# adaLN block: later modulation vectors by four row sums in column groups and a spread over memory

## Chip, core and metric

The kernel runs on one core of a Trainium2 chip. The metric is device time in microseconds. Each engine of the core works through its own instruction stream in order: TensorE (PE for its products, PEld for its weight loads), VectorE (DVE), ScalarE (ACT), GpSimd (POOL) and SyncE (SP), which here issues nearly all transfers (DMAs). Streams wait for one another through semaphores.

## The reference

```python
x = A_x                                               # 1 x 2048 x 512, float32
mod = (_silu(c) @ w_mod).reshape(c.shape[0], 6, 1, -1)  # c: 1 x 512, w_mod: 512 x 3072
sa, ca, ga, sb, cb, gb = (mod[:, i] for i in range(6))
h = _layernorm(x, axis=-1) * (1 + ca) + sa
x = x + ga * _A_ref(h, A_wqkv, A_wo)                  # 32 heads of 16, softmax attention, then wo
h = _layernorm(x, axis=-1) * (1 + cb) + sb
x = x + gb * _B_ref(h, B_w1, B_b1, B_w2)              # 512 -> 1792, mish, 1792 -> 512
```

Six modulation vectors of 512 come out of one row-by-matrix product. `sa` and `ca` (numbers 0 and 1) are needed at once; the other four (2 `ga`, 5 `gb`, 3 `sb`, 4 `cb`) only later, and they are what is changed here.

## The kernel before

**Stages.** A prologue loads x, makes vectors 0 and 1, normalises, transposes and starts the q, k, v products. Then comes the attention, 512 steps (`T`) written out by hand in `step(t)`: 32 iterations (4 blocks of 512 queries by 8 groups of 4 heads) of 16 steps, one for each block of 128 keys. The row maxima run 20 steps (`PRO`) ahead of the scores. A step puts on PE four score products (L587, exponentiated by ACT at L590), four products for maxima (L538, reduced by DVE at L540), a share of a larger product that is cut into halves of 64 rows (L138), and at its end the four products of probabilities and values of two steps before, `pv` (L605, eight instructions, since a float32 product is two). Scores and maxima go through a ring of six PSUM banks. After the steps a tail finishes the last block.

**Order.** Everything is in program order on its engine; there is no scheduler. `at(h, f)` hangs work on half step h (two to a step), which sets its place in the program order of each engine, not a time. `units` are products fed into the steps; `specials` are done whole in one place: `do_specials` emits a special's products between the step's score products and its `pv`, and its `fin` one half step later. The built program also makes each transfer of SP wait until the eighth transfer before it has landed.

**The later vectors.** `order = (2, 5, 3, 4)`; call them the first to the fourth. For each, `mod_load` (L696) loads two halves of its columns of `w_mod` (128 x 4 x 256, 512 KB) into two buffers (`hl`, `wm`), and POOL multiplies by silu(c) and adds the four blocks of rows (`sums`, L703 to L705), which leaves 128 x 256 values to be summed over the partitions. `mod_unit` (L709) does that on PE, at L131. For a gate (2, 5) it multiplies a 128 x 128 block of ones with each half, so that every partition has the whole vector, and ACT copies it to `gates` (L722). For 3 and 4 it takes each 128 columns as weights and ones as a single moving column, so that the vector lies over the partitions, and DVE copies it to `modc` (L724, L726). `queue_mod` chains the four: the special of a vector is ready 6 half steps after the place of its second `sums`; its `fin` calls `first_mods`, which issues both loads of the next vector, with the `sums` 7 and 9 half steps on. After the fourth, `start_preps` takes over the two buffers and scales and splits the later weights; the gates are read there (L737), `modc` in the second half of the block (L922, L1146).

The names in the profile: `wm` are the loads, `ring` the banks, `qscr`, `kscr`, `vscr` scratch tensors in memory for q, k and v, `sm`, `od`, `rc` the sums and rows of a finished iteration (`evac`, L613), `mt` the rows of maxima.

Of the kernel before, what the change touches and what calls it, by code (L numbers as in the profile page):

```python
# [8 lines left out]
F32 = mybir.dt.float32  # L9
F32R = mybir.dt.float32r  # L10
AF = mybir.ActivationFunctionType
# [7 lines left out]
def adaln_block(ctx: ExitStack, tc: tile.TileContext, x, wqkv, wo, w1, b1, w2, c, w_mod, out):  # L19
    nc = tc.nc  # L20
    P = 128
    S, D = x.shape[1], x.shape[2]
# [3 lines left out]
    DK = D // P  # L26
# [27 lines left out]
    dram = ctx.enter_context(tc.tile_pool(name="dram", bufs=1, space=DRAM))  # L54
# [18 lines left out]
    ones = cst.tile([P, 1], F32, name="ones")  # L73
# [9 lines left out]
    modc = cst.tile([P, 4, DK], F32, name="modc")  # L83
    sil = cst.tile([P, DK], F32, name="sil")
    b1c = cst.tile([P, FT], F32, name="b1c")
    gates = [cst.tile([P, D], F32, name=f"gate{i}") for i in range(2)]

    def dap(t, off, ap):
        return bass.AP(tensor=t.tensor, offset=t.offset + off, ap=ap)
# [36 lines left out]
    def mm(acc, l, r, start, stop):  # L126
        pe_queue.append((acc, l, r, start, stop))
# [27 lines left out]
    def ring(w=1):  # L155
        if w == 2 and ring_at[0] % 2:
            ring_at[0] += 1
        if kept and ring_at[0] % NRING == NRING - 1:
            ring_at[0] += 1
        b = ring_at[0] % NRING  # L160
        ring_at[0] += w
        return ring_t[:, b, :] if w == 1 else ring_t[:, b:b + 2, :]
# [41 lines left out]
    def at(h, f):  # L204

        hooks.setdefault(h, []).append(f)
# [121 lines left out]
    with ExitStack() as es:  # L328
# [121 lines left out]
        for i in range(2):  # L450
            row = lp.tile([P, D], F32, tag="hf", name="row", bufs=6)
# [159 lines left out]
    st, mst = {}, {}  # L611
# [84 lines left out]
    def mod_load(i, h):  # L696

        w = pw.tile([P, DK, 2 * P], F32, tag="hl", name="wm", bufs=2)
        nc.sync.dma_start(w, w_mod[:, i * 2 * P:(i + 1) * 2 * P].rearrange("(k p) m -> p k m", p=P))
        mst["wm", i] = w  # L700

        def sums():
            nc.gpsimd.tensor_mul(w, w, sil[:, :, None].to_broadcast([P, DK, 2 * P]))  # L703
            nc.gpsimd.tensor_add(w[:, 0:2], w[:, 0:2], w[:, 2:4])
            nc.gpsimd.tensor_add(w[:, 0], w[:, 0], w[:, 1])  # L705
            mst["row at", i] = h + 7
        at(h + 7, sums)

    def mod_unit(v):  # L709

        gate = v in (2, 5)
        acc, rows = ring(), [mst.pop(("wm", 2 * v + o))[:, 0] for o in range(2)]
        for o, row in enumerate(rows):
            if gate:
                mm(acc[:, o * 2 * P:(o + 1) * 2 * P], ones.to_broadcast([P, P]), row, True, True)
            else:
                for m in range(2):
                    mm(acc[:, 2 * o + m:2 * o + m + 1], row[:, m * P:(m + 1) * P], ones, True, True)

        def fin(h):  # L720
            if gate:
                nc.scalar.copy(gates[(v - 2) // 3], acc)  # L722
            elif v == 4:
                nc.vector.tensor_scalar_add(modc[:, v - 1, :], acc[:, :DK], 1.0)  # L724
            else:
                nc.vector.tensor_copy(modc[:, v - 1, :], acc[:, :DK])  # L726
        return fin

    def prep_unit(h, third, scr, src, gate):
# [666 lines left out]
    def planned(i, a, tag):  # L1396
        _, kind, sl, args = plan[i]
        unit = v_unit(sl, a, tag) if kind == 2 else qk_unit(kind, sl, a, tag)

        def fin(h):  # L1400
            if a == args[-1]:
                if i + 2 < len(plan):
                    d = 4 if h > 0 else 1
                    split_at[i + 2] = LATE_SPLIT.get(i + 2, h + d)
                    at(split_at[i + 2], lambda: slice_split(*plan[i + 2][1:3], hi_eng="p" if h > 0 else "a"))
                if i + 3 < len(plan):
                    at(LATE_LOAD.get(i + 3, h + 7), lambda: slice_load(*plan[i + 3][1:3]))
            unit(h)
            if (kind, sl, a) == (2, 0, NKC - 1):
                at(max(0, h + 2), lambda: first_mods(max(0, h + 2)))  # L1410
            if i + 1 == len(plan) and a == args[-1]:
                mst["qkv"] = h // 2 + 3
        return fin

    at(-2 * PRO, lambda: slice_load(*plan[2][1:3]))
    order = (2, 5, 3, 4)

    def first_mods(h, j=0):
        for o in range(2):
            mod_load(2 * order[j] + o, h + 2 * o)  # L1420

    def queue_mod(j):
        def make():
            put = mod_unit(order[j])

            def fin(h):
                put(h)
                if j + 1 < len(order):
                    first_mods(h, j + 1)
                else:  # L1430
                    start_preps(h + 2)
            return fin

        queue_special(lambda: mst.get(("row at", 2 * order[j] + 1), 4 * T) + 6, make)
# [110 lines left out]
```

## Time and profile before

| | |
|---|---|
| median of 3 runs | 1696.19 us (1695.32 to 1696.70) |
| the profiled execution | 1695.12 us, its span 1693.1 us |
| PE, DVE, ACT, POOL busy | 99%, 85%, 80%, 49% of the span |
| products of the four vectors (L131) start at | 123.93, 148.19, 172.28, 196.50 us |
| transfers over the span | 238.44 MB, 141 GB/s |

A row of a timeline gives start, length, engine, line, operation, tiles and count, and in brackets the idle time before it with what ended it. A row of the chain of waits gives the start, the length and the group that the end hung on. Lines such as L131 are lines of the kernel before.

### The profile page before, as it was taken

What the parts mean: (1) busy time and instruction counts of PE and PEld (TensorE: products, weight loads), DVE (VectorE), ACT (ScalarE), POOL (GpSimd) and SP (SyncE); (2) the same over time, 40 slices, a digit from 0 to 9 for tenths busy, and PEclk for the clock granted to TensorE, in tenths of its full rate; (3) what the DMA queues carried; (4) which work ended last, traced back from release to release, by engine and by line L of the source; (5) the groups of instructions that cost most, each with busy time, mean ns of one, the idle gap of its engine ahead of it and who ended that gap; (6) DMA issues with size and microseconds to landing.
All of it is one profiled execution on the core that took longest, in us unless ns stands there. A gap on an engine that the chain in (4) does not pass through costs nothing.

```text
span 1693.1 us, 33733 instructions
## 1 busy us (share of the span) xinstructions
PE 1670.7 (99%) x12406; PEld 922.2 (54%) x12406; DVE 1443.6 (85%) x2371; ACT 1356.1 (80%) x2610; POOL 822.3 (49%) x843
## 2 busy tenths in 40 slices
PE   7999999999999999999999999999999999999999
PEld 5755665555445455555555455555555445555587
DVE  8888888888889898888889898888889888884377
ACT  6257777777778988888888998888888988888674
POOL 7555224665313564555323564556323565555443
PEclk9999999999999999999999999999999999999999
DMA  7877546777755443434355534534354433433261
GB/s 248 264 241 202 130 131 186 225 222 215 225 161 142 107 100 87 125 82 131 88 139 148 118 76 94 140 75 128 83 147 123 130 93 77 143 107 129 76 230 63
DMA packets 114029, 238.44 MB, mean 141 GB/s; under 512 B 23824, under 2 KB 49424, under 8 KB 107912
## 3 DMA queue, kind: packets, MB, share of 16 engines
q1 hardware_dynamic: 113864, 236.28, 49.4%
q8 instruction: 98, 1.61, 0.4%
q14 instruction: 67, 0.55, 0.1%
HBM read 179.95 MB, written 51.44 MB: 137 GB/s over the span
## 4 chain that ended last, share of the span: by engine, by line
PE 91%; DVE 4%; ACT 3%; DMA 1%; issue 1%; POOL 1%; SPq 0%; ACTq 0%; DVEq 0%; POOLq 0%
PE bk L605 29%; PE ring L587 22%; PE ring L538 20%; PE bk L138 10%; PE bk L131 3%; PE ring L131 2%; DVE mx L540 2%; PE ring L1214 2%; ACT pr L590 1%; PE ring L552 1%; DMA qa<-mt 0%; DMA xt<-in_A_x 0%; PE ring L917 0%; PE ring L567 0%; PE ring L138 0%
## 5 line engine op out<-in xcount | busy, mean ns | idle before, releaser
L540 DVE TENSOR_REDUCE mx<-ring 128x1 f32<-128x512 f32 x1968 | 1222.1, 681 | 151.7 <-PE ring L538 136.4
L590 ACT ACTIVATE pr<-ring 128x512 f32<-128x512 f32 x2048 | 1078.3, 603 | 207.8 <-PE bk L138 117.9
L538 PE MATMUL ring<-ka,qa 64*128 64x512 f32 x1968 | 818.6, 429 | 1.7 <-ACT pr L590 1.1
L587 PE MATMUL ring<-qa,ka 64*128 64x512 f32 x2048 | 760.1, 402 | 4.3 <-ACT pr L590 2.6
L605 PE MATMUL bk<-pr,vg 128*32 128x512 f32 x4096 | 545.0, 604 | 0.0
L538 PEld LDWEIGHTS ring<-ka,qa 64*128 64x128 f32 x1968 | 350.5, 184 | 327.4 <-DVE mx L540 250.8
L587 PEld LDWEIGHTS ring<-qa,ka 64*128 64x128 f32 x2048 | 373.6, 184 | 199.2 <-DVE mx L540 115.2
L138 PE MATMUL bk<-h,w 64*128 64x512 f32 (+1 forms) x1080 | 278.6, 391 | 0.0
L138 PE MATMUL bk<-w,a_h 64*128 64x512 f32 x632 | 210.7, 413 | 0.0
L138 PEld LDWEIGHTS bk<-h,w 64*128 64x128 f32 x1080 | 178.3, 184 | 9.5 <-ACT pr L590 1.5
L605 PEld LDWEIGHTS bk<-pr,vg 128*32 128x32 f32 x4096 | 80.7, 108 | 136.1 <-issue 126.6
L138 PE MATMUL bk<-w,a_l 64*128 64x512 f32 x316 | 124.2, 393 | 0.0
L138 PEld LDWEIGHTS bk<-w,a_h 64*128 64x128 f32 x632 | 106.9, 184 | 2.7
L973 POOL TENSOR_TENSOR y<-yd,y 128x512 f32<-128x512 f32 x44 | 56.9, 1293 | 89.6 <-ACT yd L972 84.7
L807 POOL TENSOR_SCALAR qq<-ee 128x512 f32<-128x512 f32 x25 | 15.6, 624 | 168.9 <-ACT ee L801 168.9
L823 POOL TENSOR_TENSOR qq<-qq,rr 128x512 f32<-128x512 f32 x42 | 54.3, 1292 | 83.8 <-ACT rr L817 83.6
L809 POOL TENSOR_TENSOR hb<-hb,ee 128x512 f32<-128x512 f32 x42 | 54.1, 1289 | 82.3 <-DVE ee L805 80.4
L138 PE MATMUL bk<-w,o_hl 64*128 64x512 f32 x288 | 79.1, 404 | 0.0
L100 POOL TENSOR_TENSOR a_l<-hb,a_h 128x512 fp32r<-128x512 f32 x53 | 72.2, 1363 | 4.4
L97 POOL TENSOR_SCALAR qh<-qf 128x512 fp32r<-128x512 f32 x27 | 16.8, 623 | 88.7 <-ACT qf L261 69.7
L138 PEld LDWEIGHTS bk<-w,a_l 64*128 64x128 f32 x316 | 58.3, 185 | 2.9
L138 PE MATMUL bk<-h_h,wl 64*128 64x512 f32 x168 | 56.9, 420 | 0.0
(222 smaller groups left out, 1916.8 us busy)
## 6 DMA issues: line engine op xcount, KB each, us to landing
ka<-kscr SPq DMA_DIRECT2D x124, 384.0 KB
w<-w2scr SPq DMA_DIRECT2D x56, 512.0 KB
w<-w1scr SPq DMA_DIRECT2D x46, 512.0 KB
vg<-vscr SPq DMA_DIRECT2D x32, 552.0 KB
qa<-qscr SPq DMA_DIRECT2D x124, 100.0 KB
kscr<-qh SPq DMA_DIRECT2D x16, 512.0 KB
qscr<-qh SPq DMA_DIRECT2D x32, 256.0 KB
w2scr<-hl SPq DMA_DIRECT2D x14, 512.0 KB
```

What stands on the lines that cost most here:

```text
L100: (nc.gpsimd if eng == "p" else nc.vector).tensor_sub(lo, src, hi.bitcast(F32))
L131: nc.tensor.matmul(acc, l, r, start=start, stop=stop)
L138: i = nc.tensor.matmul(acc, l[64 * g:64 * g + 64], r[64 * g:64 * g + 64], start=start and not then, stop=bool(stop and then))
L538: nc.tensor.matmul(pm, qt[64 * s:64 * s + 64, qs * P:(qs + 1) * P], kt[64 * s:64 * s + 64, kb * TB:(kb + 1) * TB], start=True, stop=True)
L540: nc.vector.tensor_reduce(out=mxs[n][:, s, 4 * j + qs, kb:kb + 1], in_=pm, op=ALU.max, axis=AX.X)
L587: nc.tensor.matmul(p_, kt[64 * s:64 * s + 64, kc * P:(kc + 1) * P], qt[64 * s:64 * s + 64, :], start=True, stop=True)
L590: e = nc.scalar.activation(pr, p_, AF.Exp, scale=SCALE)
L605: nc.tensor.matmul(accs[n][32 * h:32 * h + 32, :], vgs[n][:, o:o + 32], pts.pop((t, h)), start=(kc == 0), stop=(kc == 15))
L809: (nc.vector if tail else nc.gpsimd).tensor_mul(hb, hb, ee)
L823: nc.gpsimd.tensor_mul(qq, qq, rr)
L973: nc.gpsimd.tensor_add(y[i], yd, y[i])
L1214: nc.tensor.matmul(po[i // 2][:, i % 2, :], l[:, s], w[:, r, :], start=(f == 0 and j == 0), stop=(f == FT - 1 and j == 2))
```

## The change

All four vectors are now summed in the same way: four products with a 128 x 32 block of ones, each with 128 columns, put their results side by side into the four groups of 32 partitions of one bank. ACT copies the 128 x 128 result into the second weight buffer (`modt`), for number 4 with one added. Two half steps later one row of each group (4 x 512 bytes) is stored to a scratch tensor in memory; five half steps after `fin` a second transfer reads it back, to all 128 partitions for a gate, or element by element into a column of `modc`. The second buffer is thereby in use until the store has read it, and the second load of the next vector is put 4 half steps later than before; the place of its `sums` stays where it was. In the built program PE, POOL and DVE keep their order otherwise, ACT has two copies more, DVE two fewer, SP eight transfers more.

```diff
+    mscr = dram.tile([4, DK, P], F32, name="mscr")
...
     def mod_unit(v):
-        gate = v in (2, 5)
-        acc, rows = ring(), [mst.pop(("wm", 2 * v + o))[:, 0] for o in range(2)]
-        for o, row in enumerate(rows):
-            if gate:
-                mm(acc[:, o * 2 * P:(o + 1) * 2 * P], ones.to_broadcast([P, P]), row, True, True)
+        acc, ws = ring(), [mst.pop(("wm", 2 * v + o)) for o in range(2)]
+        rows, modt = [w[:, 0] for w in ws], ws[1][:, 1, :P]
+        for c in range(DK):
+            mm(acc[32 * c:32 * c + 32, :P], ones.to_broadcast([P, 32]), rows[c // 2][:, c % 2 * P:(c % 2 + 1) * P], True, True)
+
+        def fin(h):
+            if v == 4:
+                nc.scalar.activation(modt, acc[:, :P], AF.Identity, bias=ones)
             else:
-                for m in range(2):
-                    mm(acc[:, 2 * o + m:2 * o + m + 1], row[:, m * P:(m + 1) * P], ones, True, True)
-
-        def fin(h):
-            if gate:
-                nc.scalar.copy(gates[(v - 2) // 3], acc)
-            elif v == 4:
-                nc.vector.tensor_scalar_add(modc[:, v - 1, :], acc[:, :DK], 1.0)
-            else:
-                nc.vector.tensor_copy(modc[:, v - 1, :], acc[:, :DK])
+                nc.scalar.copy(modt, acc[:, :P])
+            dst = mscr[v - 2]
+
+            def spread():
+                if v in (2, 5):
+                    nc.sync.dma_start(gates[(v - 2) // 3], dap(dst, 0, [[0, P], [1, D]]))
+                else:
+                    nc.sync.dma_start(modc[:, v - 1, :], dst.rearrange("k p -> p k"))
+
+            at(h + 2, lambda: nc.sync.dma_start(dst, modt[::32, :]))
+            at(h + 5, spread)
         return fin
...
     def first_mods(h, j=0):
-        for o in range(2):
-            mod_load(2 * order[j] + o, h + 2 * o)
+        mod_load(2 * order[j], h)
+        at(h + 4, lambda: mod_load(2 * order[j] + 1, h + 2))
```

## The prediction

> **What bounds the kernel now.** I read the page first, then the chain of waits around the four places that change, then the timelines of POOL and SP there.
>
> ```profile
> span 1693.1 us, 33733 instructions
> PE 1670.7 (99%) x12406; PEld 922.2 (54%) x12406; DVE 1443.6 (85%) x2371; ACT 1356.1 (80%) x2610; POOL 822.3 (49%) x843
> PE 91%; DVE 4%; ACT 3%; DMA 1%; issue 1%; POOL 1%; SPq 0%; ACTq 0%; DVEq 0%; POOLq 0%
> ```
>
> PE is busy throughout and carries 91% of the chain; so what PE is spared or made to wait in a step moves the end by as much. The chain around the first vector, with one ordinary step on either side:
>
> ```profile
> 121.04 0.99 PE bk L605 x8
> ...
> 123.93 1.10 PE ring L131 x4
> 125.03 0.99 PE bk L605 x8
> ...
> 127.87 1.00 PE bk L605 x8
> ```
>
> From one `pv` to the next an ordinary step takes 127.87 - 125.03 = 2.84 us; the step with the vector takes 3.99, longer by its 1.10 us of L131 and little else. The second, third and fourth cost nearly the same:
>
> ```profile
> 148.19 1.09 PE ring L131 x4
> ...
> 172.28 1.02 PE ring L131 x8
> 173.30 1.00 PE bk L605 x8
> ...
> 196.50 1.02 PE ring L131 x8
> ```
>
> Together 4.23 us lie on the path; that is all that the new products can save.
>
> **The products.** Each vector now takes four products of 128 columns in four column groups, eight instructions. The nearest row is `pv` itself, eight instructions in the same groups with 512 columns, 0.99 us on the chain. A quarter of that is 0.25 us, the lower bound. The upper bound is the same number of 128-column instructions that share nothing:
>
> ```profile
> L684 PE MATMUL ring<-ident,wide 128*64 128x128 f32 x8 | 1.1, 279 | 0.0
> ```
>
> 1.1 us, which would be no gain. I take 0.35, close to `pv`: its form is the same, and 0.1 is added for the issue, because the third product has a wait of its own for the second `sums`. Saved: 0.75 + 0.74 + 0.67 + 0.67 = 2.83 us, between 0 and 3.2.
>
> **The copies.** ACT loses two long copies and gets four short ones, DVE loses two:
>
> ```profile
> L722 ACT COPY gate<-ring x2: 616/622/627, 125.2 to 149.5; 128x512 f32<-128x512 f32 x2
> L922 ACT ACTIVATE hf<-ring,modc x48: 450/464/484, 518.0 to 1297.5; 128x128 f32<-128x128 f32 x48
> L724 DVE TENSOR_SCALAR modc<-ring x1: 163/163/163, 197.6 to 197.6; 128x4 f32<-128x4 f32 x1
> L737 POOL TENSOR_TENSOR hl<-hl,gate x18: 1270/1286/1299, 292.7 to 450.8; 128x512 f32<-128x512 f32 x18
> ```
>
> At the 128 x 128 price of L922, four copies are 1.86 us against 1.24 before. Both engines have room beside PE (80% and 85%), so nothing reaches the path: 0, at worst 0.46 in each of the last two vectors' steps if that room is gone. The spreads have some 100 us and more before the gates (292.7) and `modc` (518.0) are first read: 0 both ways.
>
> **The moved load.** This is what decides. The second load of the next vector now waits on SP until the store of the vector before has landed, since the store reads the same buffer; what is queued behind it on SP waits too. For the third vector, before (SP's timeline, and a load's size from the transfers' list; then POOL's timeline):
>
> ```profile
> 149.56 0.94 SPq L699 DMA_DIRECT2D wm<-in_w_mod  x2
> ...
> 157.83 0.57 SPq L271 DMA_DIRECT2D qscr<-ql  x1
> 161.03 0.59 SPq L630 DMA_DIRECT2D sm<-ot  x1
> ...
> 172.92 0.93 SPq L699 DMA_DIRECT2D wm<-in_w_mod  x2
> ...
> wm<-in_w_mod SPq DMA_DIRECT2D x3, 512.0 KB
> ```
>
> ```profile
> 157.90 1.89 POOL L703 TENSOR_TENSOR wm<-wm,sil 128x1024 f32<-128x1024 f32 x1 [4.78 <-PE ring L538]
> ...
> 161.92 1.89 POOL L703 TENSOR_TENSOR wm<-wm,sil 128x1024 f32<-128x1024 f32 x1
> ...
> 165.25 0.74 POOL L705 TENSOR_TENSOR wm<-wm 128x256 f32<-128x256 f32 x1
> 177.03 1.90 POOL L703 TENSOR_TENSOR wm<-wm,sil 128x1024 f32<-128x1024 f32 x1 [11.04 <-DMA wm<-in_w_mod]
> ```
>
> Both loads went out at 149.56; POOL had the first at 157.90 (8.3 us: a backlog), the second by 161.92, and finished its `sums` at 165.99 (4.07 us of work), 6.3 us before PE wanted them at 172.28. With empty queues a load takes 177.03 - 172.92 = 4.1 us. In the new order the store of the second vector stands right behind qscr<-ql on SP. How long does a transfer there take?
>
> ```profile
> SPq L641 <- DMA qscr<-ql: 1.0, 1, 1.0
> SPq L630 <- DMA wm<-in_w_mod: 2.6, 1, 2.6
> L641 SPq EVENT_SEMAPHORE  x30: 17/17/17, 169.0 to 1558.9; - x30
> ```
>
> These are waits of SP between 147 and 178 us. The last wait ended at 169.0, when qscr<-ql landed, 11.2 us after its issue; and sm went out (161.03) when the second load had landed. The queue of the transfers is drained in order, and it was full:
>
> ```profile
> DMA  0169699799999999999999765655665799930100
> GB/s 0 43 195 316 151 211 240 243 265 214 137 162 124 199 345 351 378 173 175 139 186 217 148 176 170 202 158 202 227 227 202 225 284 306 291 98 6 12 0 0
> ```
>
> That is 147 to 173 us in slices of 0.65: no gap until about 170. So the small store lands where qscr<-ql did, less what the second load, now behind it, no longer takes ahead of it: 512 KB are 1.5 us at the 351 GB/s of the fastest slices, and about 3.1 by the two landings (157.9 and 161.0). The store lands at 169.0 - 1.5 to 3.1 = 165.9 to 167.5, say 166.8. The load follows, 4.1 us: 170.9. `sums`, 4.07: 175.0. PE is there at 172.28 less the 1.49 saved at the first two vectors: 170.8. It stands in front of the third product for 4.2 us, with `pv`, the next scores and thereby ACT and DVE behind it. The last two products take some 0.2, `pv` starts at 175.2 instead of 173.30: 1.9 us late. The fourth vector gives 0.67 back. Sum: +1.3 us; by the bounds of the store's landing +0.4 to +2.0. Since the stall ends when the load says, what the products save at the first two vectors is swallowed by it; at 1.1 us a vector the sum would be +2.4, at 0.25 it would be +1.1.
>
> The other three hold. First: its store does not stand in the way of a load of its own; its second load only goes out two places later. POOL's rows for the first two vectors, and two of SP's:
>
> ```profile
> 117.97 1.90 POOL L703 TENSOR_TENSOR wm<-wm,sil 128x1024 f32<-128x1024 f32 x1
> ...
> 121.31 0.73 POOL L705 TENSOR_TENSOR wm<-wm 128x256 f32<-128x256 f32 x1
> ...
> 139.45 1.90 POOL L703 TENSOR_TENSOR wm<-wm,sil 128x1024 f32<-128x1024 f32 x1
> ...
> 125.60 0.80 SPq L312 DMA_DIRECT2D qa<-qscr  x2
> ...
> 141.26 2.67 SPq L576 DMA_DIRECT2D qa<-mt  x4
> ```
>
> POOL took it up at 117.97 only because it had other work, and ended 1.9 us before PE came at 123.93. Second: the second `sums` started at 139.45, 8.7 us before PE at 148.19. Its load now waits for the first store, behind the transfers issued from 125.60 on; by the same reckoning it lands within a us of 139.45. Margin some 3 us. Fourth: from 172.92 on the queue is nearly empty; load, store, load give POOL its data at about 185, PE comes at 196.50. Cost 0 in all three, up to 2 each if a margin is wrong.
>
> Behind the waiting load on SP stands sm, for whose data DVE divides:
>
> ```profile
> 170.41 0.24 DVE L640 RECIPROCAL rc<-sm 128x16 f32<-128x16 f32 x1
> ```
>
> sm now lands behind the load, at about 171.5, and DVE, which would be there at 168.9, waits 2.6 us, PE with it. That wait lies inside the 4.2 us and is not added.
>
> The profiled execution took 1695.12 us (its span and 2.0 around it); +1.3 makes 1696.4. The median of the runs is 1.07 above that execution: 1697.5.
>
> **Rivals.** *The store overtakes the backlog.* It has four pieces of 512 bytes, on few of the transfer engines. If these are ahead of the others, it lands at about 160, the load joins the backlog and lands at 168 at the latest; `sums` end at 172.1, the stall is 1.3: -2.83 + 1.3 = -1.5 us, 1694.7; with no stall at all -2.8, 1693.4. Against: qscr<-ql took 11.2 us in that queue. [...] Only if the products cost no more than 0.25 and nothing stalls does it come near -3.2.
>
> *PE loses its clock in the stall* (slower). At the start, after long idleness, the same form ran slower:
>
> ```profile
> L448 PE MATMUL ring<-wma,sil 128*32 128x512 f32 x16 | 3.6, 1061 | 9.2 <-DVE sil L363 9.2
> L605 PE MATMUL bk<-pr,vg 128*32 128x512 f32 x272 | 36.2, 605 | 0.0
> ```
>
> 1061 ns against 605, though the row of the granted clock is full over the whole span:
>
> ```profile
> PEclk9999999999999999999999999999999999999999
> ```
>
> If two waits of over 2 us within 6 bring that back for the 3.6 us that it lasted there at least, the price is some 1.8, for 7 us 3.5: +3.1 to +4.8, take +4: 1700.2. [...]
>
> *A second transfer comes late* (slower): the rows of maxima for the second iteration, issued from 141.26 us, now stand behind the second vector's load, a vg load and the gate. If they miss the scores by 2 to 3 us, or the third vector's store lands 2.5 later than said, the end is +3.3 to +4.3: 1700.
>
> **Numbers.** What a measurement can tell from no change is about 0.2%, 3.4 us. Forecast (stall at the third vector, -0.5 to +3) 0.55; overtaking or no stall 0.17; clock 0.12; second late transfer 0.16. Faster by over 0.2% needs the products at their floor and no stall: 0.06 out of the second case. Slower by over 0.2%: 0.10 of the clock, 0.12 of the late transfer, 0.05 of the forecast's tail, 0.27. Within: 0.67. The range leaves out the far end of both sides: 1693.3 (no stall) to 1701.0.
>
> **What would show it.** Right: L131 about 0.35 us on the chain for the first, second and fourth vector; at the third a POOL wait for the load ending at about 171 and a PE wait for `sums` of about 4 us (shared with DVE waiting for sm); from there on ordinary steps. Wrong: L131 near 1 us (the products do not share), no PE wait near 171 to 175, a wait at another vector, matmuls of 1 us after the stall, or ACT named before the scores of the last two vectors' steps.

## The result, and the profile after

| | median | lowest to highest | ratio to before, 95% interval |
|---|---|---|---|
| before | 1695.8 us (15 runs) | 1694.16 to 1699.32 | 1 |
| changed | 1699.74 us (15 runs) | 1697.41 to 1702.0 | 1.0022 (1.0015 to 1.0029) |

The change costs 3.9 us by the medians; 1697.5 was predicted, with a range up to 1701.0. The profiled execution took 1699.35 us, its span 4.5 us more than before. One of the twelve runs of one kernel below (product later) took 3750.89 us and is left out of its median. The page after:

```profile
span 1697.6 us, 33767 instructions
PE 1668.8 (98%) x12414; PEld 919.7 (54%) x12414; DVE 1444.2 (85%) x2369; ACT 1355.9 (80%) x2612; POOL 820.7 (48%) x843
PE 91%; DVE 4%; ACT 2%; DMA 2%; POOL 1%; issue 1%; SPq 0%; ACTq 0%; POOLq 0%; DVEq 0%
```

PE is busy for 1.9 us less (1670.7 before) in a span 4.5 us longer: it stands still for some 6 us more. The chain of waits around the first vector (start, length, group; L132 and L606 are L131 and L605 of before):

```profile
121.18 1.02 PE bk L606 x8
...
124.10 0.42 PE ring L132 x8
124.52 0.86 PE bk L606 x8
...
127.22 1.00 PE bk L606 x8
```

Two steps take 127.22 - 121.18 = 6.04 us; before, 127.87 - 121.04 = 6.83. The products went from 1.10 to 0.42, and `pv` behind them is 0.13 shorter: 0.79 us saved at this vector. So what the change is built of works, and the loss is elsewhere. SP's timeline, from the first vector to the third:

```profile
127.67 0.58 SPq L730 DMA_DIRECT2D mscr<-wm  x1
137.05 0.37 SPq L700 DMA_DIRECT2D wm<-in_w_mod  x1
...
158.98 0.57 SPq L272 DMA_DIRECT2D qscr<-ql  x1
161.67 0.52 SPq L730 DMA_DIRECT2D mscr<-wm  x1
168.60 0.40 SPq L700 DMA_DIRECT2D wm<-in_w_mod  x1
169.10 0.60 SPq L631 DMA_DIRECT2D sm<-ot  x1
```

and the waits of SP between 120 and 172 us (total, times, longest):

```profile
SPq L700 <- DMA mscr<-wm: 15.1, 2, 8.7
```

Both second loads stand on SP until the store of the vector before has landed: 8.7 us the first time, 6.4 the second. The store is 2 KB; it lands 9.4 and 6.9 us after its issue. Both times the transfer engines have just run dry: their busy share is 0.02 between 136 and 137 us and 0.00 in the next, 0.10 between 168.0 and 168.6 and 0.00 from there to 169.5. What follows, in POOL's timeline and then in PE's (in brackets the idle time before, and what ended it):

```profile
141.33 1.89 POOL L704 TENSOR_TENSOR wm<-wm,sil 128x1024 f32<-128x1024 f32 x1 [2.49 <-PE ring L539]
...
172.37 1.89 POOL L704 TENSOR_TENSOR wm<-wm,sil 128x1024 f32<-128x1024 f32 x1 [6.55 <-DMA wm<-in_w_mod]
...
175.68 0.72 POOL L706 TENSOR_TENSOR wm<-wm 128x256 f32<-128x256 f32 x1
```

```profile
170.10 0.39 PE L588 MATMUL ring<-qa,ka 64*128 64x512 f32 x1
170.13 0.40 PE L139 MATMUL bk<-wh,h_l 64*128 64x256 f32 x2
173.22 0.79 PE L588 MATMUL ring<-qa,ka 64*128 64x512 f32 x1 [2.69 <-DVE mx L541]
...
176.45 0.43 PE L132 MATMUL ring<-wm,ones 128*32 128x128 f32 x2 [1.86 <-POOL wm L706]
```

PE stands still from 170.5: first for DVE, then, after 1.4 us of scores and the first two products, for the `sums`. The waits between 165 and 186 us name what held DVE:

```profile
DVE rc L641 <- DMA sm<-ot: 3.3, 1, 3.3
...
PE ring L588 <- DVE mx L541: 2.7, 1, 2.7
```

That is sm, which stood behind the waiting load on SP. Then the chain behind the stall:

```profile
168.60 3.61 DMA wm<-in_w_mod
172.37 1.90 POOL wm L704
...
176.45 0.43 PE ring L132 x2
176.88 0.21 PE bk L606
177.09 1.71 PE bk L606 x6
178.80 0.72 PE ring L588
...
181.06 0.99 PE bk L606 x8
...
183.95 1.00 PE bk L606 x8
```

From 181.06 to 183.95 a step takes 2.89 us again, but the one before took 181.06 - 176.88 = 4.18, with matmuls at half rate (1057 ns for one of `pv`, 605 before): 1.3 us more. The windows show it; the number behind POOL's is the granted clock:

```profile
170.00:172.00 2.00, 0.53 (x8) 0.33 (x4) 0.00 (x0) 1.52 (x4) 0.00 (x0) 1.00 0.97 279
172.00:174.00 2.00, 0.78 (x4) 0.34 (x6) 1.63 (x4) 0.00 (x0) 1.63 (x1) 0.71 0.53 170
174.00:178.00 4.00, 2.14 (x18) 0.70 (x16) 0.96 (x2) 0.86 (x2) 2.24 (x3) 0.50 0.75 187
178.00:180.00 2.00, 2.00 (x14) 1.18 (x12) 0.41 (x1) 0.44 (x1) 0.00 (x0) 0.59 0.95 307
180.00:182.00 2.00, 2.00 (x24) 1.03 (x21) 2.00 (x4) 1.72 (x4) 1.46 (x1) 1.00 0.20 71
```

Stretches with one clock throughout read 1.00 (170 to 172, 180 to 182) or 0.50 (174 to 178). With these two values alone, a mean of 0.71 in two microseconds puts the fall at 172.84, and 0.59 the return at 179.64: by this estimate 6.8 us at half rate. Of these PE had work in 173.2 to 174.6, which the stall covered, and from 176.45 on, which it did not.

### The profile page after: what moved, and what is told of

Read it like the earlier page. It is cut to its first block, busy times and chain, and to the rows that moved or that the text cites. A ratio compares the mean times of both kernels' runs of the same rounds, so it can differ in the third digit from the quotient of the medians.

```text
span 1697.6 us, 33767 instructions
## 1 busy us (share of the span) xinstructions
PE 1668.8 (98%) x12414; PEld 919.7 (54%) x12414; DVE 1444.2 (85%) x2369; ACT 1355.9 (80%) x2612; POOL 820.7 (48%) x843
## 4 chain that ended last, share of the span: by engine, by line
PE 91%; DVE 4%; ACT 2%; DMA 2%; POOL 1%; issue 1%; SPq 0%; ACTq 0%; POOLq 0%; DVEq 0%
PE bk L606 29%; PE ring L588 22%; PE ring L539 19%; PE bk L139 10%; PE bk L132 3%; DVE mx L541 2%; PE ring L1219 2%; PE ring L132 2%; ACT pr L591 1%; PE ring L553 1%; DMA xt<-in_A_x 0%; PE ring L922 0%; DMA qa<-mt 0%; PE ring L568 0%; DMA qscr<-ql 0%
## 5 line engine op out<-in xcount | busy, mean ns | idle before, releaser
L606 PE MATMUL bk<-pr,vg 128*32 128x512 f32 x4096 | 546.4, 605 | 0.0
L606 PEld LDWEIGHTS bk<-pr,vg 128*32 128x32 f32 x4096 | 81.5, 108 | 135.6 <-issue 126.0
```

Of the source, the lines that this page charges most:

```text
L606: nc.tensor.matmul(accs[n][32 * h:32 * h + 32, :], vgs[n][:, o:o + 32], pts.pop((t, h)), start=(kc == 0), stop=(kc == 15))
```

## Experiments

The theory: the products save what was said; the loss is the wait of a load for the store out of the same buffer, and the clock that falls in the stall. Rivals: the later place of the load alone; the new transfers themselves; the products.

| kernel | median | ratio to before, 95% interval | first to fourth vector |
|---|---|---|---|
| gate tile as staging, load late | 1695.77 us | 1.0000 (0.9991 to 1.0009) | 71.85 us |
| gate tile as staging, both loads together | 1693.64 us | 0.9986 (0.9978 to 0.9995) | 70.24 us |
| the same on a second chip | 1693.92 us | 0.9987 (0.9978 to 0.9996) | 70.23 us |
| changed, stores issued by ACT | 1696.31 us | 1.0004 (0.9995 to 1.0013) | 72.49 us |
| before, with store and late load | 1700.93 us | 1.0032 (1.0020 to 1.0043) | 78.76 us |
| changed, sm ahead of the load | 1703.87 us | 1.0049 (1.0037 to 1.0061) | 79.84 us |
| the same, PE kept busy | 1700.16 us | 1.0032 (1.0021 to 1.0043) | 77.94 us |
| changed, product later | 1698.50 us | 1.0019 (1.0010 to 1.0028) | 85.05 us |
| product later and sm ahead | 1694.15 us | 0.9992 (0.9984 to 1.0001) | 81.73 us |
| gate tile, products four times | 1695.46 us | 0.9998 (0.9989 to 1.0007) | 72.19 us |
| gate tile, no gate store or spread | 1692.67 us | 0.9982 (0.9973 to 0.9990) | 70.21 us |
| changed, on that second chip | 1699.55 us | 1.0022 (1.0011 to 1.0033) | 77.42 us |

Rows 1, 2, 4 and 5 were measured on one chip, rows 6 to 9 on another, and the rest on the one called the second chip; each ratio is to the kernel before on the same chip (1695.49, 1695.2 and 1695.54 us). The last column is the start of the fourth vector's product less that of the first in the profiled execution: 72.57 before, 77.31 in the changed kernel. It leaves out what executions of one kernel differ by ahead of the first vector and behind the fourth. In rows 8 and 9 the third product stands later, so that they compare only with each other.

**The wait and the place of the load.** First the buffer alone:

```diff
-        rows, modt = [w[:, 0] for w in ws], ws[1][:, 1, :P]
+        rows = [w[:, 0] for w in ws]
+        modt = gates[(v - 2) // 3][:, :P] if v in (2, 5) else ws[1][:, 1, :P]
```

> The changed kernel, but the vectors 2 and 5 are staged for their store in the gate tile that their spread fills later, not in the second buffer: no load waits for a store any more in front of the second and third vector, while the second load stays four half steps late. Theory A (the wait of the load on the store makes the loss): no stall at the third vector, 1692.7 us (1695.8 less 3.1). Theory B (the later place of the load is itself enough, since the load now stands behind qscr<-ql in a full queue): the load lands at about 169.5, the sums end at about 173.5, PE stands 2 to 3 us: 1694.5 to 1696. Theory C (stores and spreads on the transfer queue cost by themselves): near 1699.

Measured 1695.77: theory B by the time, though PE stands for less than the 2 to 3 us said. Its chain and its PE timeline:

```profile
160.96 7.34 DMA wm<-in_w_mod
```

```profile
172.53 0.30 PE L132 MATMUL ring<-wm,ones 128*32 128x128 f32 x2 [1.26 <-POOL wm L706]
```

Without the wait the load goes out 7.6 us earlier than in the changed kernel (160.96, not 168.60), but into the full queue: it takes 7.34 us instead of 3.61, and PE still stands for 1.3 us. So most, not all, of the loss was the wait; the place takes a part. By the last column, 5.5 us of the way from 77.31 to the 70.24 of the next kernel come with the wait (and the clock that falls in it), 1.6 with the place. Then the place too:

```diff
-        at(h + 4, lambda: mod_load(2 * order[j] + 1, h + 2))
+        if j < 3:
+            mod_load(2 * order[j] + 1, h + 2)
+        else:
+            at(h + 4, lambda: mod_load(2 * order[j] + 1, h + 2))
```

> As the run before, and both loads of the second and third vector are issued together as in the kernel before. Theories A and B: no PE wait near 171 to 176, the products keep their saving of about 0.79 us a vector: 1692.7 us, ratio to before 0.998. Theory C: the transfers of the stores and spreads cost what the products save or more: 1695.8 or above.

Measured 1693.64, faster than both kernels; on the second chip 1693.92:

> The kernel with the gate tile as staging and both loads together once more, on the chip of these runs: 1.8 to 3.1 us below before, faster than both kernels.

> The changed kernel itself, on the chip of these runs, to stand beside the others: 3.5 to 5 us over before; its excess over the kernel with the gate tile as staging and both loads together is the price of the wait, by the two profiles 7.5 us.

The changed kernel on that chip came to 1699.55, so wait, place and clock together are worth 5.6 us there, less than the 7.5 of the two profiles. In the chain of the second run the third vector has no stall:

```profile
172.33 0.42 PE ring L132 x8
172.75 0.86 PE bk L606 x8
```

The centre of the gain, 1.6 to 1.9 us, is short of the 3.1 that four vectors at 0.79 make; the intervals (up to 3.7) hold it. The profiles have all of it: from the first to the fourth vector both take 2.33 us less than before, three times 0.78. What the profile on the second chip lacks beside the first (a span of 1693.2 against 1690.1) was lost elsewhere: 1.65 ahead of the first product (125.60 against 123.95) and 1.46 behind the fourth. The reverse, the kernel before with nothing but the store, which makes the load wait, and the later load:

```diff
+            at(h + 2, lambda: nc.sync.dma_start(mscr[v - 2], ws[1][::32, 1, :P]))
...
-        for o in range(2):
-            mod_load(2 * order[j] + o, h + 2 * o)
+        mod_load(2 * order[j], h)
+        at(h + 4, lambda: mod_load(2 * order[j] + 1, h + 2))
```

> The kernel before, its products and copies untouched, with only a store of one stretch of the second buffer to memory (never read) and the second load four half steps later. Theory A/B (the stall is all that costs): the sums of the third vector end at 175 to 176.5, PE, there at 172.3, stands 3 to 4 us, and about 1.2 us go to a lower clock: 1699.5 to 1701.5. Theory C (the new products or the spreads cost): close to 1695.8.

Measured 1700.93, 5.4 us over before. The stall is enough by itself, without the new products and without a spread (by the last column +6.2).

**Does the queue of SP make the store late?** The store moved to ACT:

```diff
-            at(h + 2, lambda: nc.sync.dma_start(dst, modt[::32, :]))
+            at(h + 2, lambda: nc.scalar.dma_start(dst, modt[::32, :]))
```

> The changed kernel with the stores of the vectors issued by ACT and not by SP; shared buffer and late load stay. If the store is late only because it stands behind the backlog of its own queue, it lands within 3 us of its issue (about 163), the second load of the third vector goes out then, behind what is still queued, lands at about 169 to 170 and the stall is 2 to 3 us without the half clock: 1695 to 1696.5. If the engines of the transfers are shared so that the queue does not matter, the store lands at 166 to 168.5 as before and the time is 1699 to 1700.

The time came out as said (1696.31), the reason did not. ACT's timeline, SP's timeline and SP's waits (145 to 172 us):

```profile
150.61 0.51 ACTq L730 DMA_DIRECT2D mscr<-wm  x1
```

```profile
160.08 0.57 SPq L272 DMA_DIRECT2D qscr<-ql  x1
160.76 0.42 SPq L700 DMA_DIRECT2D wm<-in_w_mod  x1
```

```profile
SPq L272 <- DMA mscr<-wm: 3.0, 1, 3.0
```

The store left ACT at 150.61, long before the 161.67 of the changed kernel, as ACT doesn't stand in line on SP; SP's wait for it (at a transfer that reuses its completion semaphore) ended at 160.08, when qscr<-ql went out. So it still took some 9.5 us on a queue that carries only the four stores. What was gained goes with the earlier issue: the load went out at 160.76 and not at 168.60. Why the store takes as long on that queue was not shown.

**Two waits, one on top of the other?** The load for the third vector one half step later, so that sm stands ahead of it:

```diff
-        at(h + 4, lambda: mod_load(2 * order[j] + 1, h + 2))
+        at(h + (5 if j == 2 else 4), lambda: mod_load(2 * order[j] + 1, h + 2))
```

> The changed kernel with the second load of the third vector issued one half step later, so that sm (and the gate's spread) stand ahead of the load that waits for the store, not behind it. Theory D (DVE's wait for sm lies inside the stall, as the prediction said): DVE divides without a wait, PE does its scores at once and then stands in one piece of about 5 us for the sums; the sums end at about 177 and the time stays at 1699.5 to 1700.5. Theory E (the two waits add up): PE loses 2.7 us less, 1697.

DVE's wait is gone and nothing is gained: theory E falls. PE's timeline and the windows:

```profile
177.48 0.43 PE L132 MATMUL ring<-wm,ones 128*32 128x128 f32 x2 [6.48 <-POOL wm L706]
```

```profile
172.00:174.00 2.00, 0.00 (x0) 0.00 (x0) 0.00 (x0) 0.00 (x0) 0.61 (x1) 0.85 0.86 243
174.00:178.00 4.00, 0.52 (x8) 0.48 (x12) 0.00 (x0) 0.00 (x0) 3.27 (x3) 0.50 0.93 240
178.00:182.00 4.00, 4.00 (x24) 2.24 (x18) 1.38 (x3) 1.43 (x3) 3.13 (x2) 0.50 0.26 61
182.00:184.00 2.00, 2.00 (x17) 1.01 (x13) 1.25 (x2) 1.23 (x3) 0.78 (x2) 0.59 1.03 361
```

One gap of 6.5 us instead of two; the `sums` end about 1 us later, as the load took 5.19 us and not 3.61; the gate's spread now goes ahead of it, which is the likely reason. But 1703.87 is more than theory D gave: the clock is at half from 173.4 to 183.6, and 6.2 us of that are work (177.48 to 183.6), so that some 3.1 us are lost. That this is the clock, the next run tests:

```diff
         for c in range(DK):
+            for _ in range(26 if v == 3 and c == 2 else 0):
+                mm(acc[:, P:2 * P], ident, ident, True, True)
```

> As the run before, and PE does 26 idle products of the identity (128 x 128, some 0.16 us each, 4.2 us) into unused columns of the bank while it would wait for the sums, so that it is not idle. [...] Theory G (the half clock costs nothing that the stall has not cost already): the same time as the run before, within 0.5 us.

```profile
178.90 0.30 PE L132 MATMUL ring<-wm,ones 128*32 128x128 f32 x2 [1.31 <-POOL wm L706]
179.31 0.86 PE bk L606 x6
```

These are PE's timeline and, below it, the chain's `pv`. With useless work in the gap (the 26 products took 6.07 us, 0.23 each) the granted clock reads 1.00 in every microsecond from 166 to 188, `pv` takes 0.86 again, and the time is 3.7 us lower (1700.16 against 1703.87), although the `sums` came 1.4 us later in this profile. Theory G falls. The half rate costs more here than the 1.3 us of the changed kernel, as it had lasted 10.2 us there and not 6.8. The medians are of 5 and 6 runs and their intervals overlap; the last column has 1.9 us less with `sums` 1.4 us later, 3.3 together, near the 3.1 reckoned.

**Nobody waits.** The buffer, the load and the store stay as in the changed kernel, and the third vector's product is taken up later:

```diff
-        queue_special(lambda: mst.get(("row at", 2 * order[j] + 1), 4 * T) + 6, make)
+        queue_special(lambda: mst.get(("row at", 2 * order[j] + 1), 4 * T) + (14 if j == 2 else 6), make)
```

> The changed kernel with the product of the third vector taken up eight half steps later (about 11 us), after its sums are there; the load still waits for the store and sm still stands behind it. No PE wait for the sums any more. Theory H (DVE's late division then holds PE by itself): one gap of about 2.7 us near 170.5 to 173.2, 1696.3, and up to 1698 if the clock drops. Rival (the gap closes itself since the ring of score banks has room): 1693.6, as with the gate tile as staging.

```profile
173.34 0.49 PE L588 MATMUL ring<-qa,ka 64*128 64x512 f32 x1 [3.12 <-DVE mx L541]
```

```profile
170.00:174.00 4.00, 0.88 (x9) 0.36 (x11) 1.51 (x4) 1.28 (x4) 1.43 (x1) 1.00 0.75 229
174.00:178.00 4.00, 4.00 (x41) 2.22 (x35) 3.56 (x6) 2.60 (x5) 2.48 (x3) 1.00 0.80 211
```

Theory H: the wait for the `sums` is gone, and sm by itself holds PE for 3.1 us, with the clock at 1.00; 1698.50, a little more than the 1696.3 to 1698 said. So each of the two waits is enough by itself, and each hides the other. With both edits:

> Both: product eight half steps later and sm ahead of the waiting load. Shared buffer, late load, stores and spreads are all there, only nobody waits for them. Theory A: 1693.6, as with both loads issued together and the gate tile as staging. If the spreads, the late fourth vector or the later weight preparations cost something, above 1695.

1694.15, and 3.3 us less than the run before in the last column: no wait of PE, no loss, with shared buffer, late load, stores and spreads all in place. It is the second version below before, by its centre (its interval ends at 1.0001).

**What the parts cost when nothing waits.** Products four times over:

```diff
-        for c in range(DK):
+        for c in 4 * list(range(DK)):
```

> The kernel with the gate tile as staging and both loads together, with the four products of each vector made four times over (32 instructions in place of 8). If the products lie on the path at the 0.42 us that the chain shows, three more sets at four vectors add 12 x 0.42 = 5.0 us, perhaps less, since the first of a set hides the weight loads of the next: 4 to 5 us over the same kernel with one set. If they lie beside other work, it stays within 1 us of it.

A miss: 1.5 us by the medians, where 4 to 5 were said. The chain at the first vector:

```profile
125.38 1.08 PE ring L132 x32
```

Three more sets cost 0.66 us, 0.22 each, not 0.42: 2.6 us for all (1.96 over the three vectors of the last column). That weight loads run beside products shows in the changed kernel: PEld loads those of `pv` from 124.21 to 124.47 us, while the products of the vector run from 124.10 to 124.52. And without the store and the spread of the gates, which are set to 1 at the start, so that this kernel leaves a part of the computation out:

```diff
+    for g in gates:
+        nc.gpsimd.memset(g, 1.0)
...
-            at(h + 2, lambda: nc.sync.dma_start(dst, modt[::32, :]))
-            at(h + 5, spread)
+            if v in (3, 4):
+                at(h + 2, lambda: nc.sync.dma_start(dst, modt[::32, :]))
+                at(h + 5, spread)
```

> The kernel with the gate tile as staging and both loads together, without the store and the spread of the two gate vectors (the gates are set to 1 once at the start, so that part of the computation is left out; the two column vectors keep theirs). If the transfers cost nothing: the same time, within 1 us. If the 512 KB that they move in the full queue, or SP's wait for the store ahead of the spread, cost something: 1 to 3 us faster.

1.25 us below the same kernel with them, at the edge of the second answer; the intervals overlap (0.9973 to 0.9990, and 0.9978 to 0.9996). From the first to the fourth vector, where these transfers lie, the kernels take 70.21, 70.23 and 70.24: they cost nothing there. A cost of up to a microsecond elsewhere is open.

## Why the prediction was right, and where it was off

- **The products** (0.35 on the chain): 0.42, with `pv` 0.13 shorter. 0.79 saved, 0.75 said. Four sets show the price of a further one at 0.22, close to the lower bound of 0.25; the rest, 0.20, each vector pays once.
- **Copies and spreads** at nothing: no wait at another vector, and no ACT or DVE copy, appears on the chain. The gates' transfers cost nothing between the vectors; elsewhere it is not settled below a microsecond.
- **The second vector** (load within a us of 139.45): POOL began at 141.33, 1.9 us late; the margin of 3 held it.
- **The store of the second vector** (166.8): the term that was mis-sized. The load behind it went out at 168.60. The store lands with the end of the backlog, as reckoned (in the kernel before, the landings for which SP waited came in the order of issue: the second load at 161.0 us, qscr<-qh at 166.3 and 167.6, qscr<-ql at 169.0): 168.60 - 158.98 = 9.6 us after that was issued, against 11.2 before, 1.6 less, the lower end of the 1.5 to 3.1 of which the middle was taken: 0.6 of the miss. The other 1.15 is that qscr<-ql itself went out at 158.98 and not at 157.83; I had left its issue where it was. In SP's waits from 156.5 us on, it goes out when a ka<-kscr has landed, where before a wm load was waited for too; why that was later is open. The load then took 3.6 us (4.1 said), the `sums` 4.0 (4.07 said). `pv` started at 176.88 instead of 175.2.
- **DVE's wait for sm inside the stall**: right, shown by the run with sm ahead (no gain) and by the run with the later product, where it comes out and costs its own 3.1.
- **The clock** was kept as a rival with 0.12, and priced at +4 in all. It is no rival of the forecast: it fell inside the stall that was forecast (0.50 from 172.84 on), and it cost 1.3 us here. The 7 us in its price stood on no run; the runs showed 6.8 us of half rate here and in the kernel before with store and late load, and 10.2 with sm ahead of the load. One of the signs named for being wrong, matmuls of 1 us after the stall, did appear: those of `pv` took 1057 ns between 176.5 and 177.7 us.
- **The sum**: +1.3, and 1.7 for the store, and 1.3 for the clock, less 0.1 for the fourth vector: +4.2. The spans give +4.5, the medians +3.9. So these two terms, 3.0 us together, are what lies above the forecast: 2.9 by the profiled executions, 2.2 by the medians, since the changed kernel's median lies 0.39 above its execution and not the 1.07 that was carried over.
- **The range**: the stall, its place and its cause are as forecast, its size is not. 1699.74 lies at the prices of two rivals (1700 for a store that lands 2.5 us late, 1700.2 for the clock), and each came in part: the store was 1.8 late. The change of 0.22% lies on the edge of the 0.2% within which 0.67 of the chances stood. That the time is in the range is due to the room left at the slow end for these two.
- **The store overtakes the backlog**: no, on SP's queue (it landed 9.4 and 6.9 us after its issue) or on ACT's (some 9.5). (The 1.5 us for 512 KB go by 351 GB/s; the row has a slice of 378, which makes 1.4 and changes nothing.)

## What to carry to other kernels

A small store is not quick because it is small: on SP's queue it was done when the backlog of transfers was, 6.9 and 9.4 us later, and on ACT's it took some 9.5 us all the same. Do not let a load wait for one, nor put either into a full queue; stage in a buffer that is free anyway (here the tile that the result goes to in the end). When two waits overlap, take both away, or little or nothing comes of it, and price a stall of PE at its length and, where the clock falls in it, at most half of the time of the half-rate work behind it (3.2 us of such work in the changed kernel, for which the step behind the stall took 1.3 us more).

## What the runs showed of the hardware

The fall of the clock did not need one long pause here. In the changed kernel it fell at 172.84, with PE idle only since 170.53 (2.3 us), and in the kernel before with store and late load after pauses of 1.2 and some 0.8 us with work between (a mean of 0.86 puts the fall at 175.44, PE idle since 174.64); yet a single pause of 3.12 us left it at 1.00. PE's timeline and the windows of the kernel before with store and late load:

```profile
173.38 0.50 PE L588 MATMUL ring<-qa,ka 64*128 64x512 f32 x1 [1.16 <-DVE mx L541]
...
174.06 0.58 PE L132 MATMUL ring<-ones,wm 128*128 128x1 f32 x4 [0.18 <-DVE mx L541]
```

```profile
172.00:174.00 2.00, 0.72 (x5) 0.20 (x3) 1.48 (x4) 1.24 (x4) 1.51 (x1) 1.00 0.25 52
174.00:176.00 2.00, 0.58 (x4) 0.52 (x4) 1.11 (x2) 0.57 (x1) 1.84 (x3) 0.86 1.00 271
```

Half rate lasted 6.8 us in the changed kernel, 6.8 in this one (a mean of 0.94 over 182 to 184 puts its end at 182.24) and 10.2 with the gap of 6.5. The length of a pause alone does not tell them apart: 2.3 us, and 1.2 and 0.8 with work between, cost the clock, and 3.12 us did not. What decides was not shown. The scatter of several microseconds between runs is not explained by these falls: the kernel before has it too (1694.16 to 1699.32).
